# Second MoE: the last group of f made wholly of pairs with seven products

## The chip, the cores and the metric

The program runs on one core of a Trainium2 chip. The metric is the device time of one execution in microseconds (us); lower is better. TensorE (PE in the rows) multiplies matrices into PSUM, VectorE (DVE), ScalarE (ACT) and GpSimd (POOL) work elementwise, and SyncE (SP) issues DMA transfers. PEld is TensorE's loading of weights, which overlaps its matmuls.

## The reference, cut to what matters

Attention with a decay bias makes 2304 tokens of 512 features. Two MoE layers with one expert each follow:

```
def _moe_ref(x, w_in, w_out):
    h = np.maximum(x @ w_in, 0.0)
    return h * h @ w_out                   # 512 -> 2048 -> 512

def _moe2_ref(x, w_in, w_out):
    h = x @ w_in
    g = h * np.cos(h)
    return g @ w_out                       # 512 -> 2048 -> 512
```

The change lies in the second MoE. All is in 32-bit floats at the interface.

## The kernel before, in words

The 2048 hidden columns of the second MoE are 16 chunks f of 128. The 2304 tokens are five blocks j: four of 512 and one of 256 (j = 4). Every 32-bit number that enters a matmul there is split into a high and a low half of 16 bits, and each product is made in three passes (high by high, high by low, low by high).

The chunks are taken in three groups (`GROUPS`). For each group, all blocks are run through one after the other: for each (block, f) the first product makes h in PSUM (`m2_g1`, tile hp, 12 matmuls of 512 columns, or of 256 in the last block), `m2_cos` and `m2_sin` make the cosine (ScalarE: a, kf; VectorE: kf; ScalarE: the sine into a), `m2_mul` multiplies h by it (VectorE), `m2_high` and `m2_rest` split the result into gh (ScalarE) and gl (VectorE), and two items later `m2_g2` multiplies by the second weights and adds up in PSUM (tiles o, one for each 128 tokens). At the end of a group, `m2_g2` evicts each o: the first group's are scaled and stored, the second group's are added by VectorE to what is stored, and the last group's likewise for even tiles, while for odd tiles ScalarE copies into os and GpSimd adds os to the stored part. A group's next o of the same place needs the eviction of the one before.

In the last group (from f = 9), the first f of each block is made as above (an f-item), and the six others as three pairs in the four blocks of 512 (`unit`, from `PAIR0`). A pair makes the first product of two f's in seven products of half the size (`prod`, `PROD`; each six matmuls of 256 columns) in place of the eight that two f's have, as Strassen's and Winograd's methods do: on sums and differences of four quarters of the weights (made once, in `pair_high`: four tensor operations of VectorE into a tile sums, then the high and the low halves) and of the activations (made for each block in `t_make`, a step at each `t_tick`: differences by VectorE, high halves by ScalarE, low halves by VectorE). The products land in three PSUM banks, which share three buffers with hp. ScalarE copies banks into hs (`snap`), VectorE adds banks to hs (`join`). Between the products, `unit` weaves the second products of earlier f's (`out_part`, first and second from a queue `fifo`), and the sines, products and splits of the pair before. Product 5 is accumulated in the bank that `snap` has copied after product 6; product 4 is added in the bank that `join` has read after product 7.

The weights are prepared meanwhile: each chunk is loaded, clipped by ScalarE, put together from bits by two operations of VectorE (`w_bits`), squared for a scale (ScalarE), its scale made (`w_scale`), and split into high (ScalarE) and low halves (VectorE; `w_lo`). How many are taken at each item is set by rates, `P_BITS` first and then `LATE_BITS`; the scales of a group (`group`) must stand before its first f. The order of the instructions on each engine is the order in which this code writes them (the schedule is manual), and each engine takes its own in that order.

Of the kernel before, what the change touches and what calls it, by code (L numbers as in the profile page):

```python
# [8 lines left out]
F32 = mybir.dt.float32  # L9
# [11 lines left out]
DM = 512  # L21
DFF = 2048
KD = DM // 128
NF = DFF // 128
BT = 256
# [2 lines left out]
MAGIC = 12582912.0  # L28
SCALE = 204
TINY = 2.0 ** -96  # L30
GROUPS = ((0, 4), (4, 9), (9, 16))
PAIR0 = 10
T_FROM = 20
LATE_BITS = 0.62
RAWS = 6
NB2 = 5
LAG = (3, 5)
G2LAG = 2
PASSES = ((0, 0), (0, 1), (1, 0))
# [93 lines left out]
def attention_moe_moe_kernel(  # L133
# [18 lines left out]
    nc = tc.nc  # L152
# [38 lines left out]
    p2q = []  # L191
    prog = [0]
    wq = []
    for f in range(NF + G2LAG):
        wq += [(0, f, 0)] if f < NF else []
        wq += [(0, f - G2LAG, 1)] if f >= G2LAG else []
    wq += [(1, f, a) for f in range(PAIR0) for a in range(2)]
    wq += [(1, f + m, a) for f in range(PAIR0, NF, 2) for a in range(2) for m in range(2)]
    spot = {x: j for j, x in enumerate(wq)}

    def home(m, f, a):
# [52 lines left out]
    def v_own(b):  # L254
# [24 lines left out]
        out=ident, in_=ident, pattern=[[-1, 128]], compare_op=ALU.not_equal, fill=1.0,  # L279
# [23 lines left out]
    def store_ones(eng, n0, n1):  # L303
# [10 lines left out]
        out=mask[:, 384:512], in_=mask[:, 384:512], pattern=[[-1, 128]], compare_op=ALU.is_ge,  # L314
        fill=-8.0e9, base=0, channel_multiplier=1,
    )
    for t in early[2:]:
        early_ones(t, nc.gpsimd)
    nc.vector.tensor_scalar(
        out=cs[0:32, 0:S], in0=cs[0:32, 0:S], scalar1=0.0, scalar2=8.0, op0=ALU.max, op1=ALU.mult  # L320
    )
    cc = []
    for x0, x1, t in ((0, BT, "xh"), (BT, S, "xl")):
        nc.vector.tensor_tensor_scan(
            out=c8[0:32, x0:x1], data0=cs[0:32, x0:x1], data1=cs[0:32, x0:x1],
# [51 lines left out]
    for n, (u, b, h, q0, rws, o, nq, nk, nl) in enumerate(heads):  # L377
        q = q0
# [611 lines left out]
    def split(j):  # L990
        return wq[j][0] == 1 and wq[j][1] >= PAIR0 and wq[j][2] == 0

# [17 lines left out]
    def pair_high(j, m):  # L1010

        f = wq[j][1]
        t = wp.tile([128, 2, 512], F32, tag=home(1, f, 0), name="wt3")
        t = t.rearrange("p a c -> p (a c)").bitcast(F16).rearrange("p (e x c) -> p e x c", e=2, x=4)
        sc = sm["wsc"][:, 2 * f:2 * f + 1]
        if m == 0:
            q = p2q[0].tile([128, KD, BT], F32, tag="yr", bufs=2, name="sums")
            x, y = (wst[j + n][1].rearrange("p (a c) -> p a c", a=2) for n in range(2))
            for n, (u, v, op) in enumerate((
                (y[:, 0], y[:, 1], ALU.add), (q[:, 0], x[:, 0], ALU.subtract), (x[:, 0], y[:, 0], ALU.subtract),  # L1020
                (x[:, 1], q[:, 1], ALU.subtract),
            )):
                nc.vector.tensor_tensor(out=q[:, n], in0=u, in1=v, op=op)
            parts = ((t[:, :, 1:3], x), (t[:, :, 0], y[:, 1]), (t[:, :, 3], q[:, 0]))
            wt[1, f, 0] = t[:, :, 1:3].rearrange("p e x c -> p e (x c)")
            pair[f] = (t, y, q)
        else:
            t0, y, q = pair[f - 1]
            parts = ((t[:, :, 0:3], q[:, 1:4]), (t[:, :, 3], y[:, 0]))
            wt[1, f, 0] = (t, t0)  # L1030
            pair[f - 1] = (t0, t)
        pair[j] = (parts, sc)
        for o, i in parts:
            nc.scalar.activation(out=o[:, 0], in_=i, func=ACTF.Copy, scale=sc)
# [20 lines left out]
    stat, part, half, sm = [], {}, {}, {}  # L1055
# [34 lines left out]
    def w_scale(j):  # L1090
# [3 lines left out]
        powers(stat[0][:, c], sm["wsm"][:, c], sm["wex"][:, c], sm["wsc"][:, c])  # L1094
        for g, (f0, f1) in enumerate(GROUPS):
            if wq[j + 1] == (1, f1 - 1, 1):
# [21 lines left out]
    def tables(g, j0, j1):  # L1118

        fs = slice(*GROUPS[g])  # L1120
        n, js = GROUPS[g][1] - GROUPS[g][0], slice(j0, j1)
        nc.vector.scalar_tensor_tensor(
# [109 lines left out]
    yr = {}  # L1232
# [12 lines left out]
    def split_y(j, a):  # L1245
        if a == 0:
            pool = p2q[0] if j < NB2 - 1 else p2q[1]
            yd[j] = [pool.tile([128, KD, blocks[j][1]], F16, tag=f"{x}{j}", bufs=1, name=x) for x in ("yh", "yl")]
# [6 lines left out]
    def load_ys(j):  # L1255
        for a in range(blocks[j][1] // BT if j < NB2 else 0):
            load_y(j, a)
# [28 lines left out]
    def moe_slot():  # L1286
# [9 lines left out]
        g2done[0] += 1  # L1296
        if k == NB1 - 1 and 2 * f >= RAWS and not (f >= PAIR0 and f % 2 == 0):
            while nw[0] < 2 * (NF + f + 1):
# [207 lines left out]
    while prog[0] < unit_done(0):  # L1506
        i = prog[0]
        x = i - FIRST_BITS
        step(bits=int((x + 1) * PROLOG_BITS) - int(x * PROLOG_BITS) if x >= 0 else 0)

    for k in range(NB1):
# [8 lines left out]
        for i in range(J):  # L1520
# [6 lines left out]
            if k == NB1 - 1:  # L1527
# [15 lines left out]
                wlim[0] = 2 * NF + max(RAWS * (i > 1), 2 * max(0, i - LOAD_LAG))  # L1543
                bits = min(2 * GROUPS[0][1], int(max(0, i - 1) * B8_BITS)) - int(max(0, i - 2) * B8_BITS)
                bits = max(0, bits)
# [41 lines left out]
    p2 = ctx.enter_context(tc.tile_pool(name="p2", bufs=1))  # L1587
# [71 lines left out]
    def m2_g2(p, j, f, pick=None):  # L1659
        t0, n = blocks[j]  # L1660
        gh, gl = hd2[j, f]
        w = wt[1, f, 1]
        first, last = (f == x for x in (GROUPS[p][0], GROUPS[p][1] - 1))
        sc = sm["osc"][:, p, j:j + 1]
        if first:
            ops.setdefault(j, {})
        for a in range(n // 128) if pick is None else pick:
            if first:
                ops[j][a] = ps2.tile([128, DM], F32, tag=f"o{a}", name=f"o{a}")
            for m, (e, x) in enumerate(PASSES):  # L1670
                nc.tensor.matmul(  # L1671
                    ops[j][a], (gh, gl)[e][:, a * 128:(a + 1) * 128], w[:, x, :],
                    start=(first and m == 0), stop=(last and m == 2),
                )
            if last:
                st = part[4 * j + a]
                if p == 1 or p and (a % 2 == 0 or j == NB2 - 1):
                    nc.vector.scalar_tensor_tensor(  # L1678
                        out=st, in0=ops[j][a], scalar=sc, in1=st, op0=ALU.mult, op1=ALU.add
                    )  # L1680
                elif p:
                    os = p2.tile([128, DM], F32, tag="os", bufs=2, name="os")
                    nc.scalar.activation(out=os, in_=ops[j][a], func=ACTF.Copy, scale=sc)
                    nc.gpsimd.tensor_tensor(out=st, in0=os, in1=st, op=ALU.add)
                elif a % 2 == 0:
                    nc.scalar.activation(out=st, in_=ops[j][a], func=ACTF.Copy, scale=sc)
                else:
                    nc.vector.tensor_scalar(out=st, in0=ops[j][a], scalar1=sc, scalar2=None, op0=ALU.mult)
            if f == NF - 1:
                for row, x, m in _pieces(t0 + a * 128, 128):  # L1690
                    nc.sync.dma_start(out=out[row:row + m, :], in_=part[4 * j + a][x:x + m])

    HB = BT
    PROD = {1: (0, 1, 0), 2: (0, 2, 1), 3: (1, 2, 2), 4: (0, 0, 6), 5: (0, 3, 3), 6: (1, 0, 4), 7: (1, 1, 5)}
# [90 lines left out]
    def unit(j, f, prev):  # L1785

        p = len(GROUPS) - 1
        w_need(2 * NF + 2 * f + 4)
# [57 lines left out]
    for j in range(NB2):  # L1846
        n = PAIR0 if j < NB2 - 1 else NF
        items += [("f", 2, j, f) for f in range(GROUPS[2][0], n)] + [("u", 2, j, f) for f in range(n, NF, 2)]
    bits0 = nw[2]
    prev = None  # L1850
    for i, (kind, p, j, f) in enumerate(items):
# [22 lines left out]
        if i >= QUIET:  # L1874
            w_squares()
            while wrest:
                x = wrest.pop(0)
# [14 lines left out]
        k = i + 1 - QUIET  # L1892
        goal = min(4 * NF, bits0 + int(max(0, min(k, PAUSE)) * P_BITS) + int(max(0, k - PAUSE - 1) * LATE_BITS))
        if i >= QUIET:
# [17 lines left out]
    while fifo:  # L1912
        m2_g2(*fifo.pop(0))
# [49 lines left out]
```

## Time and profile before

| what | us |
|---|---|
| median of three runs | 971.03 (970.65 to 972.81) |
| profiled execution | 972.91 |
| its span | 970.8 |
| TensorE busy | 937.3 (97%) |
| VectorE busy | 769.7 (79%) |
| ScalarE busy | 709.7 (73%) |
| GpSimd busy | 159.9 (16%) |

The profile is one execution on the chip. The span is the time from its first to its last instruction; the execution lies 2.1 us above it. The second MoE begins at some 595 us: its first products and second products stand in the list of costly groups as lines L1610 (hp) and L1671 (o), the pairs' products as L1762 (bank). The granted TensorE clock is at its full level in all 40 slices of the span.

### The profile page before, as it was taken

What the parts mean: (1) busy time and instruction counts of PE and PEld (TensorE: products, weight loads), DVE (VectorE), ACT (ScalarE), POOL (GpSimd) and SP (SyncE); (2) the same over time, 40 slices, a digit from 0 to 9 for tenths busy, and PEclk for the clock granted to TensorE, in tenths of its full rate; (3) what the DMA queues carried; (4) which work ended last, traced back from release to release, by engine and by line L of the source; (5) the groups of instructions that cost most, each with busy time, mean ns of one, the idle gap of its engine ahead of it and who ended that gap; (6) DMA issues with size and microseconds to landing.
All of it is one profiled execution on the core that took longest, in us unless ns stands there. A gap on an engine that the chain in (4) does not pass through costs nothing.

```text
span 970.8 us, 21039 instructions
## 1 busy us (share of the span) xinstructions
PE 937.3 (97%) x7474; PEld 726.9 (75%) x7474; DVE 769.7 (79%) x1944; ACT 709.7 (73%) x1625; POOL 159.9 (16%) x298
## 2 busy tenths in 40 slices
PE   6999999989999999999999999999999999999997
PEld 5899998988989988999989986445544456666664
DVE  6899986789798866787997375888788788798774
ACT  6799887878898767676776686677777666565553
POOL 2001123222211222222330022430000000001101
PEclk9999999999999999999999999999999999999999
DMA  8984799657998987589999679210000000112001
GB/s 246 312 271 149 168 213 227 168 145 151 200 183 191 204 195 170 134 177 174 211 215 158 217 267 362 66 44 23 1 1 1 22 1 22 49 60 67 23 22 66
DMA packets 158074, 135.38 MB, mean 139 GB/s; under 512 B 109272, under 2 KB 132128, under 8 KB 157968
## 3 DMA queue, kind: packets, MB, share of 16 engines
q1 hardware_dynamic: 147664, 123.78, 50.8%
q0 software_dynamic: 10304, 10.24, 5.2%
q8 instruction: 59, 0.97, 0.4%
q14 instruction: 47, 0.39, 0.1%
HBM read 93.91 MB, written 15.83 MB: 113 GB/s over the span
## 4 chain that ended last, share of the span: by engine, by line
PE 59%; DVE 6%; ACT 3%; issue 2%; DMA 2%; SPq 0%; DVEq 0%; ACTq 0%
PE o L1671 18%; PE hp L1610 12%; PE y L1197 11%; PE hps L1165 9%; PE bank L1762 5%; PE qkp L567 2%; PE pvs L697 2%; DVE k L415 1%; DVE sb L585 1%; DMA raw<-in_qk_dram 1%; DMA rw<-in_w_dram 1%; DMA vb<-v_d 1%; DVE wt L1678 1%; PE xps L752 0%; ACT sb L608 0%
## 5 line engine op out<-in xcount | busy, mean ns | idle before, releaser
L1197 PE MATMUL y<-gh,wt 128*128 128x256 f32 x1152 | 237.7, 289 | 0.0
L1197 PEld LDWEIGHTS y<-gh,wt 128*128 128x128 f32 x1152 | 188.6, 190 | 1.2
L1671 PE MATMUL o<-wt,gh 128*128 128x512 f16 x576 | 171.3, 379 | 1.5 <-ACT gh L1649 1.3
L1197 PE MATMUL y<-gl,wt 128*128 128x256 f32 x576 | 162.9, 283 | 0.5 <-DVE gl L1187 0.5
L1165 PE MATMUL hps<-xh,w 128*128 128x256 f16 x1152 | 142.0, 273 | 2.6 <-ACT g L1177 2.4
L1610 PE MATMUL hp<-yh,wt 128*128 128x512 f16 (+1 forms) x448 | 124.9, 348 | 0.0
L1165 PEld LDWEIGHTS <-w 128*128 128x128 f16 x1152 | 106.1, 98 | 17.8 <-issue 4.2
L1197 PEld LDWEIGHTS y<-gl,wt 128*128 128x128 f32 x576 | 109.9, 191 | 1.4 <-DVE gl L1187 0.9
L1671 PE MATMUL o<-wt,gl 128*128 128x512 f16 x288 | 109.2, 379 | 0.0
L1610 PEld LDWEIGHTS <-wt 128*128 128x128 f16 x672 | 63.9, 98 | 59.1
L1671 PEld LDWEIGHTS <-gh 128*128 128x128 f16 x576 | 56.3, 98 | 56.3 <-ACT gh L1649 1.6
L608 ACT ACTIVATE sb<-sb 128x128 f32<-128x128 f32 (+7 forms) x152 | 87.4, 575 | 4.9 <-DVE sb L585 4.3
L1177 ACT ACTIVATE g<-hps,sc 128x256 f32<-128x256 f32 x96 | 45.1, 470 | 61.3 <-PE hps L1165 59.8
L397 POOL DMA_DIRECT2D k<-ext_d x80 | 41.1, 514 | 260.2 <-PE qkp L567 159.3
L1165 PE MATMUL hps<-xh,wt 128*128 128x256 f32 x384 | 81.4, 294 | 0.3 <-ACT g L1179 0.2
L1187 DVE TENSOR_TENSOR gl<-g,gh 128x256 fp32r<-128x256 f32 x144 | 61.3, 426 | 22.8 <-ACT gh L1181 14.7
L1610 PE MATMUL hp<-yl,wt 128*128 128x512 f16 (+1 forms) x224 | 78.0, 348 | 0.0
L585 DVE CUSTOM_DVE_ANT_0 sb<-qkp,mask 128x128 f32<-128x128 f32 (+7 forms) x152 | 69.3, 456 | 5.3 <-PE qkp L552 4.3
L656 DVE SCALAR_TENSOR_TENSOR p<-sb,p 128x384 f16<-128x384 f32 (+3 forms) x120 | 66.3, 553 | 8.8 <-ACT p L650 5.6
L1635 ACT ACTIVATE a<-kf 128x512 f32<-128x512 f32 (+1 forms) x80 | 46.5, 583 | 31.4 <-DVE kf L1630 30.4
L405 ACT CAST hi<-raw 128x704 fp32r<-128x704 f32 (+2 forms) x80 | 58.8, 735 | 13.6 <-DMA raw<-in_qk_dram 7.2
L1165 PEld LDWEIGHTS hps<-xh,wt 128*128 128x128 f32 x384 | 64.5, 195 | 2.8 <-issue 1.2
(172 smaller groups left out, 2006.8 us busy)
## 6 DMA issues: line engine op xcount, KB each, us to landing
rw<-in_w_dram SPq DMA_DIRECT2D x64, 512.0 KB
raw<-in_qk_dram SPq DMA_DIRECT2D x48, 352.0 KB
yr<-y_d SPq DMA_DIRECT2D x17, 512.0 KB
raw<-in_qk_dram SPq DMA_DIRECT2D x16, 384.0 KB
v_d<-vt SPq DMA_DIRECT2D x16, 320.0 KB
vb<-v_d SPq DMA_DIRECT2D x32, 160.0 KB
vr<-in_v_dram POOLq DMA_DIRECT2D x15, 320.0 KB, 5.4
y_d<-yst SPq DMA_DIRECT2D x18, 256.0 KB
```

What stands on the lines that cost most here:

```text
L405: nc.scalar.copy(hi[:, BT - nq:BT + nk], raw[:, BT - nq:BT + nk])
L585: nc.vector.tensor_tensor_reduce(out=sb[0:r, c0:c0 + cn], in0=p[0:r, 0:cn], in1=mask[0:r, mo:mo + cn], scale=-0.125, scalar=(3.0e38 if k = ...
L608: nc.scalar.activation(out=sb[0:r, 0:w], in_=sb[0:r, 0:w], func=ACTF.Exp, scale=-1.0, bias=j["nb"], accum_out=z[0:r, ti, x:x + 1],)
L656: nc.vector.scalar_tensor_tensor(out=p[0:r, cw:cw + w], in0=sb[0:r, 0:w], scalar=PSC, in1=p[0:r, 0:w], op0=ALU.mult, op1=ALU.subtract,)
L1165: nc.tensor.matmul(hp, w[:, a, c * 128:(c + 1) * 128], (xh, xl)[e][:, c, :], start=(n == 0), stop=(n == 3 * KD - 1),)
L1177: nc.scalar.activation(out=g, in_=hp, func=ACTF.Relu, scale=hs1[:, f // 2:f // 2 + 1])
L1187: nc.vector.tensor_tensor(out=gl, in0=g, in1=gh, op=ALU.subtract)
L1197: nc.tensor.matmul(yps[k][d // 2][:, d % 2, :], w[:, a, d * 128:(d + 1) * 128], (gh, gl)[e], start=(f == 0 and n == 0 and d % 2 == 0), sto ...
L1610: nc.tensor.matmul(hp, chunk_of(w, a, c), (yh, yl)[e][:, c, :], start=(m == 0), stop=(m == 3 * KD - 1),)
L1635: nc.scalar.activation(out=a, in_=kf, func=ACTF.Sin, scale=-6.2831850)
L1671: nc.tensor.matmul(ops[j][a], (gh, gl)[e][:, a * 128:(a + 1) * 128], w[:, x, :], start=(first and m == 0), stop=(last and m == 2),)
L1762: nc.tensor.matmul(bank[b][:, 0:HB], w[:, a, wx, c * 128:(c + 1) * 128], y_side(j, yx, e, c), start=(start and n == 0), stop=(n == 5), ski ...
```

## The change

The groups are now f 0 to 3, 4 to 7 and 8 to 15. The second group so loses f = 8 (five items), and in the last group the four blocks of 512 are made of four pairs each, with no f-item; the block of 256 keeps f-items, eight of them. The weights of the pair (8, 9) are converted with the second ones first, and the rate of conversions late in the first and in the second group goes from 0.62 to 0.76 for each item. The four quarters' sums go into a buffer that they share with os; of os there is so one buffer in place of two. `PARTS` names the tiles in which the 18 results of 128 tokens are kept, since fewer chunks have a tile of that kind.

```diff
-GROUPS = ((0, 4), (4, 9), (9, 16))
-PAIR0 = 10
+GROUPS = ((0, 4), (4, 8), (8, 16))
+PAIR0 = 8
-LATE_BITS = 0.62
+LATE_BITS = 0.76
+PARTS = (*range(2 * PAIR0), 2 * PAIR0 + 1, 2 * PAIR0 + 3)
...
-    wq += [(1, f + m, a) for f in range(PAIR0, NF, 2) for a in range(2) for m in range(2)]
+    wq += [(1, f + m, a) for f in range(PAIR0, NF, 2) for a in ((1, 0) if f == PAIR0 else (0, 1)) for m in range(2)]
...
-            q = p2q[0].tile([128, KD, BT], F32, tag="yr", bufs=2, name="sums")
+            q = p2q[1].tile([128, KD, BT], F32, tag="os", bufs=1, name="sums")
...
-                st = part[4 * j + a]
+                st = part[PARTS[4 * j + a]]
...
-                    os = p2.tile([128, DM], F32, tag="os", bufs=2, name="os")
+                    os = p2.tile([128, KD, BT], F32, tag="os", bufs=1, name="os")[:, 0:2].rearrange("p a c -> p (a c)")
```

The evictions at the end of a block move within the pairs. These are ScalarE's rows around the end of the first block's last group, in the kernel before (os is the copy of an odd o; L1772 the bank copies; L1621 and L1635 make a and the sine, L1649 gh):

```order
L1772 COPY hs<-bank 128x256 x2
L1683 ACTIVATE os<-o_12233,osc 128x512
L1772 COPY hs<-bank 128x256
L1621 ACTIVATE a<-hs,hsc 128x512 x2
L1683 ACTIVATE os<-o_12261,osc 128x512
L1772 COPY hs<-bank 128x256
L1635 ACTIVATE a<-kf 128x512 x2
L1649 CAST gh<-a 128x512
```

and in the change (its lines stand one further down):

```order
L1773 COPY hs<-bank 128x256 x2
L1622 ACTIVATE a<-hs,hsc 128x512 x2
L1773 COPY hs<-bank 128x256
L1684 ACTIVATE os<-o_12082,osc 128x512
L1636 ACTIVATE a<-kf 128x512 x2
L1650 CAST gh<-a 128x512
L1773 COPY hs<-bank 128x256
L1684 ACTIVATE os<-o_12116,osc 128x512
```

Both copies to os moved: the first from behind the earlier bank copies to a place right before the two sines, the second from before them to behind the bank copy that follows gh.

The second place is VectorE early in the second group. Before, behind the product of that group's third item (L1641 is the product, L1708 and L1714 are a difference and a low half of y, L1624 kf, L1656 gl):

```order
L1641 SCALAR_TENSOR_TENSOR a<-hp_11063,gsc,a 128x512
L1708 TENSOR_TENSOR yr<-yr 128x512
L1624 SCALAR_TENSOR_TENSOR kf<-kf,a 128x512
L1656 TENSOR_TENSOR gl<-a,gh 128x512
L1641 SCALAR_TENSOR_TENSOR a<-hp_11108,gsc,a 128x512
L1714 SCALAR_TENSOR_TENSOR wt_9790<-wt_9886,ysc,wt_9790 128x512
```

and in the change the same stretch from the last of the four sums (L1024), which stand behind the same kf, to the next product (L1043 makes a pair's low halves, L982 and L986 the bits):

```order
L1024 TENSOR_TENSOR sums<-st,sums 128x256
L1657 TENSOR_TENSOR gl<-a,gh 128x512
L1043 SCALAR_TENSOR_TENSOR wt_11135<-st,wsc,wt_11135 128x512
L1043 SCALAR_TENSOR_TENSOR wt_11135<-st,wsc,wt_11135 128x256
L1043 SCALAR_TENSOR_TENSOR wt_11135<-sums,wsc,wt_11135 128x256
L982 TENSOR_SCALAR st<-st 128x512
L986 SCALAR_TENSOR_TENSOR st<-rw,st 128x512
L1642 SCALAR_TENSOR_TENSOR a<-hp_11115,gsc,a 128x512
```

The sums and the conversions of the first pair's first half, and two operations on bits, have come in between one item's kf and the next product.

## Rows read from the trace of the kernel before

**Rows 1.** Busy time by stretches: stretch, its length, engines' busy times, PEclk, DMA, GB/s.

```profile
720.00:740.00 20.00, 19.97 (x99) 8.95 (x98) 17.63 (x34) 14.01 (x26) 0.00 (x0) 1.00 0.01 1
800.00:820.00 20.00, 18.21 (x123) 11.65 (x122) 16.51 (x45) 11.63 (x26) 0.00 (x0) 1.00 0.09 27
```

**Rows 2.** Chain of waits from 770 on: start us, us, what.

```profile
772.41 2.61 PE hp L1610 x12
...
824.63 1.30 PE o L1671 x6
825.93 1.31 PE bank L1762 x12
```

**Rows 3.** Timeline, VectorE in the second group, and TensorE's second products by the chain.

```profile
703.39 0.69 DVE L1624 SCALAR_TENSOR_TENSOR kf<-kf,a 128x512 f32<-128x512 f32 x1 [1.29 <-ACT kf L1623]
...
720.16 2.72 DVE L1678 SCALAR_TENSOR_TENSOR wt<-o,osc,wt 128x512 f32<-128x512 f32 x4
...
725.18 0.15 DVE L1076 TENSOR_SCALAR wsm<-stat 128x2 f32<-128x2 f32 x1
...
725.65 0.68 DVE L1624 SCALAR_TENSOR_TENSOR kf<-kf,a 128x512 f32<-128x512 f32 x1
...
726.25 0.42 DVE L1023 TENSOR_TENSOR sums<-st 128x256 f32<-128x256 f32 x1
...
727.71 0.69 DVE L1656 TENSOR_TENSOR gl<-a,gh 128x512 f16<-128x512 f32 x1
728.31 1.15 DVE L1042 SCALAR_TENSOR_TENSOR wt<-st,wsc,wt 128x512 f16<-128x512 f32 x2
...
729.77 0.42 DVE L981 TENSOR_SCALAR st<-st 128x512 int32<-128x512 int32 x1
...
730.83 0.75 DVE L1641 SCALAR_TENSOR_TENSOR a<-hp,gsc,a 128x512 f32<-128x512 f32 x1
...
722.82 2.59 PE o L1671 x12
```

**Rows 4.** Timeline at the passage into the pairs: start us, us, engine, line, operation.

```profile
804.60 1.41 DVE L1051 SCALAR_TENSOR_TENSOR wt<-st,wsc,wt 128x512 f16<-128x512 f32 x2
...
805.92 0.48 DVE L1641 SCALAR_TENSOR_TENSOR a<-hp,gsc,a 128x256 f32<-128x256 f32 x1
...
820.47 0.37 ACT L1772 COPY hs<-bank 128x256 f32<-128x256 f32 x1
...
821.21 0.82 PE L1762 MATMUL bank<-wt,wt 128*128 128x256 f16 x6
```

**Rows 5.** Timeline of a steady pair, from its product 1 to its product 5.

```profile
895.16 0.27 PE L1762 MATMUL bank<-yh,wt 128*128 128x256 f16 x1
...
896.29 1.22 ACT L1635 ACTIVATE a<-kf 128x512 f32<-128x512 f32 x2
...
897.09 1.41 DVE L1641 SCALAR_TENSOR_TENSOR a<-hs,gsc,a 128x512 f32<-128x512 f32 x2
...
897.87 0.62 ACT L1649 CAST gh<-a 128x512 f16<-128x512 f32 x1 [0.35 <-DVE a L1641]
...
898.62 0.37 ACT L1772 COPY hs<-bank 128x256 f32<-128x256 f32 x1
...
900.38 0.82 PE L1762 MATMUL bank<-wt,wt 128*128 128x256 f16 x6
```

**Rows 6.** Timeline: evictions by os, GpSimd's adds, and VectorE beside them.

```profile
882.80 0.69 ACT L1683 ACTIVATE os<-o,osc 128x512 f32<-128x512 f32 x1 [0.98 <-PE o L1671]
...
886.17 1.27 POOL L1684 TENSOR_TENSOR wt<-os,wt 128x512 f32<-128x512 f32 x1 [1.33 <-ACT os L1683]
886.22 1.77 DVE L1630 TENSOR_TENSOR kf<-kf,a 128x512 f32<-128x512 f32 x1
...
951.39 2.50 POOL L1684 TENSOR_TENSOR wt<-os,wt 128x512 f32<-128x512 f32 x2 [29.23 <-ACT os L1683]
...
951.80 0.48 DVE L1641 SCALAR_TENSOR_TENSOR a<-hp,gsc,a 128x256 f32<-128x256 f32 x1
```

More of the change, by code (lines that the diff above doesn't have):

```diff
@@ L1690, in m2_g2 @@
                 for row, x, m in _pieces(t0 + a * 128, 128):
-                    nc.sync.dma_start(out=out[row:row + m, :], in_=part[4 * j + a][x:x + m])
+                    nc.sync.dma_start(out=out[row:row + m, :], in_=part[PARTS[4 * j + a]][x:x + m])
     HB = BT
```

## The prediction, as made before the run

> **What bounds the kernel now.** I read the busy time by stretches first. In the second MoE TensorE works without a break: 19.97 of 20 us between 720 and 740, as in nearly every stretch there; the one poor stretch is 800 to 820, with 18.21 of 20, where the second group of f ends and the pairs begin [rows 1]. So time leaves only with TensorE's columns, and comes with any wait put in front of it. The chain of waits gives the price of each piece of matmul work: an f's first product with 512 tokens is 2.61 us, twelve products of a pair 1.31 us, six matmuls of the second product 1.30 us [rows 2]. The timelines then say how much room the other engines leave, and there lie my other terms.
>
> **Columns.** In each of the four blocks of 512 tokens two f's cost 2 x 2.61 = 5.22 us of first products, and a pair costs 7 x 6 = 42 matmuls of 256 columns, 42/12 x 1.31 = 4.59 us. The pair (8, 9) so gives back 0.63 us a block, 2.5 us in all. The second products stay. The added matmul for the pair's sum of squares and the wider tables of scales are a few rows of some 0.2 us each off TensorE's path. In SP's queue two weight loads change places, long before their weights are used: nothing. The sums' own buffer takes away a sharing with the loads of y; no wait on it shows, so nothing here either.
>
> **Preparing weights in the second group.** The second group has 20 items in place of 25, and the same weights, plus one pair's sums, must be ready before it ends. On VectorE each item has its own work (a product, kf, gl), and the conversions lie between. I walk VectorE's row order of the change from a point where the trace is on time, the kf at 703.39, which waited for ScalarE [rows 3]. Steps are from one start to the next: kf 0.60 (725.65 to 726.25), the four sums 1.46 (to 727.71), gl 0.60, the pair's low halves 1.46 (728.31 to 729.77), bits 1.06 (to 730.83); a product or a low half of y 0.68 (a fourth of the 2.72 of the evictions at 720.16), a difference of y 0.60 as kf, the scales 0.47 (725.18 to 725.65). The order is now: kf, sums, gl, low halves, bits (5.18), product, low, difference (1.96), kf, gl, low halves, bits (3.72), product, low, difference (1.96), kf, gl (1.20), four evictions (2.72), bits (1.06), product, low, scales (1.83), kf, sums, gl to its end (2.75): 22.4 us, to 725.8. TensorE wants that gl as the third matmul of the second products that start at 722.82, at 722.82 + 2 x 0.22 = 723.25. It comes 2.5 us late. Before, the gl for those matmuls stood right before the evictions at 720.16, 3 us before that need, since the pair's sums and their conversions stood later in the order. From below this is 0 (if the row order overlaps more than its starts show; a walk of 42 instructions needs only 0.06 us less on each), from above 4 (two further lags of the kind). I take 2.5, the walk itself.
>
> **The passage into the pairs.** Two f-items disappear between the last weights and the first pair: the block of 256's f = 8 and the first block's f = 9. They gave VectorE time to catch up. The first pair's product 7 needs the PSUM bank that the last f leaves, so it waits for the product that the trace has at 805.92, behind two low halves of weights that take 1.41 from 804.60; the wait is between nothing and these 1.41, and I put 0.8, about the middle, as TensorE meets the rest of the weights' work where it did before. In the second pair product 5 needs a copy of the bank by ScalarE. In the trace that copy ends at 820.47 + 0.37 = 820.84 and product 5 starts at 821.21: room of 0.37 [rows 4]. In the change the second products woven in there are of the block of 256, half as long, so product 5 comes 1.3 us earlier, and an eviction of 0.66 stands before the product that the copy waits behind: 1.3 + 0.66 - 0.37 = 1.6 us. Together 2.4 us; bounds 1 and 3.5.
>
> **The three ends of a block.** In the steady pair product 1 starts at 895.16, and its sines at +1.13, product on VectorE at +1.93, gh at +2.71, bank copy at +3.46 (ends +3.83); product 5 starts at +5.22, so ScalarE may be 1.39 late [rows 5]. Before, an f-item stood between two blocks and the evictions fell behind product 5; a copy to os (0.69) did not stand before a sine of the same pair's chain that TensorE soon needs. Now it does: ScalarE's order is bank copy, os of the second tile, two sines, gh, bank copy, os of the fourth tile. The second tile is finished at +2.62 (1.31 + 1.30), handed over at +2.8, os ends +3.5, the sines +4.1 and +4.7. Then the adder on GpSimd comes in: it starts as os ends and takes 1.27. A VectorE operation with both tensors in SBUF that meets it stands until it is over: kf took 1.77 in place of the 0.69 of the like one [rows 3] and ended 0.55 after GpSimd [rows 6]; a product that reads one tensor from PSUM met another add and took its 0.48. The pairs' product reads two tensors from SBUF, as that kf does. I take it as held: add +3.6 to +4.85, product to +5.4, gh +6.0, bank copy +6.4, so product 5 is 1.15 late.
> The Trainium skill (GPSIMD Engine Reference, section 1, Specifications) says that its SBUF interfaces are shared with VectorE, with contention for operations in a two-port mode or with two SBUF inputs. By it the product is held; no row of before has that pair of operations meeting, and without it product 5 would be 0.6 late by the same walk.
> Behind it the fourth tile's os ends at +7.0, its add holds gl to +8.95, and in the first two ends a difference of y (0.69) and the join (0.42) follow, to +9.9; product 4, wanted at +7.82 (5.22 + 0.65 + 1.30 + 0.65), waits for that join: 2.1 us late. The third end has no difference of y: 1.5. The walk so gives 5.7; I take 5.0, as each wait of TensorE also gives the others time; bounds 1.5 (held by nothing) and 6.5. The last end, into the block of 256, has the two os in one buffer now, so the second waits for the first add (1.27). I assume that TensorE is not waiting for that tile yet and put nothing, with 1.3 as the upper bound.
>
> **Sum.** -2.5 + 2.5 + 2.4 + 5.0 = +7.4 us. The profiled execution took 972.91 (span 970.8), so the same with the change 980.3; the three timed runs' median is 971.03, 1.9 below it, and I forecast 978.4.
>
> **Rivals.** A: TensorE's columns decide and every wait is covered, as in nearly all stretches now. It needs ScalarE's os to be no later than its room of 1.39, and VectorE's walk to be 11% shorter. For it speaks that TensorE waits for next to nothing at 720 to 740 though VectorE is busy 17.63 of 20 us [rows 1]; against it, that the room is measured and the os alone moves the sines by 2.4. The time is 971.03 - 2.5 = 968.5; this is the end on the other side. It decides up to the point where the added waits come to 2.5 us in all.
> B: the product is not held by the add, and the walk in the second group catches up. Then 1.5 to 3 remain of the block ends: -2.5 + 0 + 2 + 2.7 = +2.2, 973.2. For it: the same 17.63 of 20 us leave some room on the mean.
> C: the change prepares too little time: further lags in the second group (up to 4) and the other upper bounds, -2.5 + 4 + 3.5 + 6.5 = +11.5, 982.5. Against it: TensorE's own delays give VectorE time back.
>
> **Chances.** Forecast 0.46, B 0.22, C 0.09, A 0.23. A change under 0.2% (1.9 us) can hardly be told from none; of A and of B some 0.04 each fall there. So faster 0.19, same 0.08, slower 0.73. The forecast's own range is 975.5 to 981. The range from 968 to 982.4 leaves out about a tenth at the lower end and half of C at the upper.
>
> **What would show it.** Right: TensorE idle over 1 us before product 5 and product 4 in the second pair of each block, behind a ScalarE order os, sine, gh; a VectorE product of 1.2 us or more beside GpSimd's add; one gap of 2 us near 725 behind gl; 3 us idle more around the first two pairs. Columns: twelve products of a pair still 1.31. Wrong: the same busy share of TensorE in all stretches from 720 on, and a span 2.5 us shorter, or gaps at places that I have not named.

## The result, and the profile after

The changed kernel takes 979.04 us (median of four runs, 978.38 to 980.78) against 971.50 for the kernel before: 1.0079 times as long, with a 95% interval of 1.0061 to 1.0098. The forecast was 978.4, and slower. The first two parts of the page after, to be held against the small table of before:

```profile
span 976.5 us, 21221 instructions
PE 933.9 (96%) x7548; PEld 730.7 (75%) x7548; DVE 780.5 (80%) x1968; ACT 713.1 (73%) x1639; POOL 160.6 (16%) x298
```

TensorE is busy 3.4 us less and the span is 5.7 us longer, so TensorE stands idle more. Where, the busy time by stretches shows (the columns are those of [rows 1], which show 720 and 800 of before):

```profile
700.00:720.00 20.00, 18.02 (x87) 7.89 (x84) 18.85 (x34) 15.55 (x30) 0.00 (x0) 1.00 0.00 1
720.00:740.00 20.00, 19.93 (x94) 8.99 (x95) 19.04 (x38) 16.72 (x32) 0.00 (x0) 1.00 0.17 53
800.00:820.00 20.00, 20.00 (x136) 13.11 (x134) 16.42 (x29) 12.73 (x24) 0.00 (x0) 1.00 0.10 30
```

VectorE is now busy about 19 of 20 us from 700 to 740, and TensorE loses 2 us there. The stretch from 800 is full, because the pairs begin at 783.57 and no longer at 809.50. The granted clock is full in all three, so the clock has no part in it. (In this execution the granted clock was 0.59 from 24 to 49 us, long before the second MoE, and full from then on.) The view of waits names TensorE's waits from 600 on in the changed kernel (line, tile, what it waited for: total, times, longest). Together they are 12 us.

```profile
PE bank L1763 <- ACT hs L1773: 5.0, 5, 1.5
PE bank L1763 <- DVE hs L1777: 1.9, 3, 0.8
PE stat L1070 <- DVE wsm L1077: 1.6, 1, 1.6
PE o L1672 <- ACT gh L1650: 1.3, 1, 1.3
PE o L1672 <- DVE wt L1679: 0.8, 1, 0.8
PE bank L1763 <- DVE a L1642: 0.5, 1, 0.5
PE o L1672 <- DVE gl L1657: 0.5, 1, 0.5
PE o L1672 <- ACT wt L1712: 0.4, 1, 0.4
```

The kernel before has 2 us:

```profile
PE o L1671 <- ACT gh L1649: 1.3, 1, 1.3
PE bank L1762 <- ACT hs L1772: 0.5, 1, 0.5
PE o L1671 <- DVE wt L1678: 0.2, 1, 0.2
```

To compare kernels I use one number by place, and call it the excess: on TensorE's timeline, the time from the start of one piece of work to the start of the next, less what the piece takes when nothing waits (twelve matmuls of a pair 1.31, six second products 1.30, twelve of these 2.59). It is some 0.16 us larger than the idle gap of the profile at each wait. The lag is the second group up to its last block (in the runs with other rates the waits in the first group are in it), the last items are those of the block of 256, the first two pairs follow, and then come the three ends of a block:

| kernel | lag | last items | first two pairs | three ends | sum |
|---|---|---|---|---|---|
| before | 0.2 | 2.0 | 0.6 | 0.7 | 3.5 |
| changed | 2.4 | 3.4 | 3.2 | 6.0 | 15.0 |

In the profiled executions the second MoE takes 375.6 us before (595.22 to 970.8) and 383.7 after (592.77 to 976.5), 8.1 more: 11.5 of excess, less 2.2 for TensorE's columns, less 1.2 between TensorE's last matmul and the end. It starts 2.45 us earlier in this execution. Between 591.7 and 595.9 that start lies anywhere in the profiles of this study, with no relation to the kernel, so the medians (7.5 us apart) are the better measure of the whole.

**The end of a block.** The timeline of the changed kernel at the end of the first long block, cut to the rows that wait or are waited for:

```profile
833.26 0.69 ACT L1684 ACTIVATE os<-o,osc 128x512 f32<-128x512 f32 x1 [1.58 <-PE o L1672]
833.85 1.14 ACT L1636 ACTIVATE a<-kf 128x512 f32<-128x512 f32 x2
834.03 1.27 POOL L1685 TENSOR_TENSOR wt<-os,wt 128x512 f32<-128x512 f32 x1 [180.18 <-ACT os L1684]
834.50 2.01 DVE L1642 SCALAR_TENSOR_TENSOR a<-hs,gsc,a 128x512 f32<-128x512 f32 x2 [1.14 <-ACT a L1636]
835.88 0.62 ACT L1650 CAST gh<-a 128x512 f16<-128x512 f32 x1 [0.89 <-DVE a L1642]
836.40 0.36 ACT L1773 COPY hs<-bank 128x256 f32<-128x256 f32 x1
836.82 0.81 PE L1763 MATMUL bank<-wt,wt 128*128 128x256 f16 x6 [0.99 <-ACT hs L1773]
837.09 2.35 DVE L1657 TENSOR_TENSOR gl<-a,gh 128x512 f16<-128x512 f32 x2
837.44 1.46 POOL L1685 TENSOR_TENSOR wt<-os,wt 128x512 f32<-128x512 f32 x1 [2.14 <-ACT os L1684]
839.97 0.41 DVE L1777 TENSOR_TENSOR hs<-bank,hs 128x256 f32<-128x256 f32 x1
840.43 0.81 PE L1763 MATMUL bank<-wt,wt 128*128 128x256 f16 x6 [0.82 <-DVE hs L1777]
```

The order of events is the forecast's: os, sines, the add on GpSimd, a pair of products that takes 2.01 in place of the 1.41 of [rows 5], gh, copy, product 5. Then the second add, two gl in 2.35, the join, product 4. In [rows 5] product 5 starts 5.22 us after product 1. Here product 1 starts at 830.46 and product 5 6.36 later.

**The second group.** The timeline of the changed kernel around its longest wait there:

```profile
714.85 2.72 DVE L1679 SCALAR_TENSOR_TENSOR wt<-o,osc,wt 128x512 f32<-128x512 f32 x4
715.64 0.59 PE L1672 MATMUL o<-wt,gh 128*128 128x512 f16 x2 [0.41 <-ACT wt L1712]
719.87 0.15 DVE L1077 TENSOR_SCALAR wsm<-stat 128x2 f32<-128x2 f32 x1
720.07 0.18 PE L1070 MATMUL stat<-wss,onesb 128*128 128x1 bf16 x1 [1.65 <-DVE wsm L1077]
722.40 0.69 DVE L1657 TENSOR_TENSOR gl<-a,gh 128x512 f16<-128x512 f32 x1
```

TensorE waits twice. At 715.64 the row names a ScalarE copy, but what o needs is its buffer: the first of the four evictions ends at 714.85 + 0.68 = 715.53. At 720.07 it waits 1.65 us for a small operation of VectorE on the sums of squares (wsm), which stands behind those evictions, two operations on bits, a product and a low half. The gl of my walk ends at 722.40 + 0.69 = 723.09. The matmul that reads it comes third in the second products that start at 722.70, at 723.1, so after these two waits it is just in time.

The matmul that waits at 720.07 is one column, the sum of squares of the second weights of f = 10 (a pair's first weights have four such matmuls at once, second weights have one each; which it is follows from their order in the code). It is no part of what the change adds. The kernel before has it as well, 5.3 us behind the end of the wsm at 725.18 [rows 3], and there it waits for nothing:

```profile
730.63 0.17 PE L1069 MATMUL stat<-wss,onesb 128*128 128x1 bf16 x1
```

**The passage into the pairs.** The timeline of the changed kernel from the last items to the second pair's product 5:

```profile
773.64 0.39 PE L1672 MATMUL o<-wt,gl 128*128 128x512 f16 x1 [0.52 <-DVE gl L1657]
777.30 2.72 DVE L1679 SCALAR_TENSOR_TENSOR wt<-o,osc,wt 128x512 f32<-128x512 f32 x4
778.10 0.59 PE L1672 MATMUL o<-wt,gh 128*128 128x512 f16 x2 [0.80 <-DVE wt L1679]
785.32 1.41 DVE L1052 SCALAR_TENSOR_TENSOR wt<-st,wsc,wt 128x512 f16<-128x512 f32 x2
786.64 0.48 DVE L1642 SCALAR_TENSOR_TENSOR a<-hp,gsc,a 128x256 f32<-128x256 f32 x1
787.18 0.81 PE L1763 MATMUL bank<-wt,wt 128*128 128x256 f16 x6 [0.53 <-DVE a L1642]
796.20 0.36 ACT L1773 COPY hs<-bank 128x256 f32<-128x256 f32 x1
796.61 0.81 PE L1763 MATMUL bank<-wt,wt 128*128 128x256 f16 x6 [1.47 <-ACT hs L1773]
```

The last two waits are the ones forecast: product 7 behind two low halves and a product, and the second pair's product 5 behind its bank copy. The first two were not: a gl behind the four sums, and evictions that VectorE comes to late.

### The profile page after: what moved, and what is told of

Its sections match the earlier page's. It is cut to its first block, busy times and chain, and to the rows that moved or that the text cites. A ratio compares the mean times of both kernels' runs of the same rounds, so it can differ in the third digit from the quotient of the medians.

```text
span 976.5 us, 21221 instructions
## 1 busy us (share of the span) xinstructions
PE 933.9 (96%) x7548; PEld 730.7 (75%) x7548; DVE 780.5 (80%) x1968; ACT 713.1 (73%) x1639; POOL 160.6 (16%) x298
## 4 chain that ended last, share of the span: by engine, by line
PE 55%; DVE 12%; ACT 4%; DMA 3%; issue 2%; DVEq 0%; POOL 0%; SPq 0%; POOLq 0%; ACTq 0%
PE o L1672 15%; PE y L1198 11%; PE hps L1166 9%; PE hp L1611 8%; PE bank L1763 7%; PE qkp L568 2%; PE pvs L698 2%; DVE wt L1679 1%; DVE gl L1657 1%; DVE a L1642 1%; DMA pt<-p 1%; DMA k<-in_qk_dram 1%; DVE k L416 1%; DVE sb L586 1%; DVE st L986 1%
## 5 line engine op out<-in xcount | busy, mean ns | idle before, releaser
L1611 PE MATMUL hp<-yh,wt 128*128 128x512 f16 (+1 forms) x384 | 104.5, 343 | 0.0
L1611 PEld LDWEIGHTS <-wt 128*128 128x128 f16 x576 | 54.7, 98 | 47.6
L1763 PEld LDWEIGHTS <-wt 128*128 128x128 f16 x672 | 65.7, 98 | 29.9 <-issue 9.9
L1611 PE MATMUL hp<-yl,wt 128*128 128x512 f16 (+1 forms) x192 | 65.9, 343 | 0.0
```

The lines of the kernel that those rows point to most:

```text
L1611: nc.tensor.matmul(hp, chunk_of(w, a, c), (yh, yl)[e][:, c, :], start=(m == 0), stop=(m == 3 * KD - 1),)
L1763: nc.tensor.matmul(bank[b][:, 0:HB], w[:, a, wx, c * 128:(c + 1) * 128], y_side(j, yx, e, c), start=(start and n == 0), stop=(n == 5), ski ...
```

## The experiments

All times are medians, each with its ratio to the kernel before on the same chip; the medians of before lay between 971.1 and 972.4. The excess is that of the profiled execution, by the places of the table above; its sum is rounded by itself.

| run | us | ratio (95% interval) | lag | last items | first pairs | ends | sum |
|---|---|---|---|---|---|---|---|
| changed kernel | 979.04 | 1.0079 (1.0061 to 1.0098) | 2.4 | 3.4 | 3.2 | 6.0 | 15.0 |
| e1_no_add | 976.07 | 1.0042 (1.0025 to 1.0059) | 2.4 | 3.4 | 3.2 | 1.9 | 11.0 |
| e2_os_late | 978.18 | 1.0066 (1.0043 to 1.0089) | 2.4 | 3.4 | 3.2 | 4.4 | 13.4 |
| e3_tfrom28 | 979.92 | 1.0081 (1.0057 to 1.0105) | 1.6 | 3.7 | 3.2 | 6.0 | 14.5 |
| e4_pair10 | 971.46 | 1.0000 (0.9984 to 1.0016) | 0.1 | 3.8 | 1.4 | 0 | 5.3 |
| e5_before_buf | 970.76 | 0.9991 (0.9976 to 1.0006) | 0.2 | 2.0 | 0.6 | 0.5 | 3.3 |
| h1_evict | 975.64 | 1.0038 (1.0024 to 1.0052) | 2.4 | 3.4 | 3.2 | 1.9 | 10.9 |
| h2_order | 976.02 | 1.0044 (1.0030 to 1.0058) | 2.4 | 3.4 | 3.1 | 2.0 | 11.0 |
| p1_pace | 978.86 | 1.0075 (1.0057 to 1.0093) | 3.2 | 1.8 | 3.3 | 6.0 | 14.3 |
| m1_first | 974.00 | 1.0028 (1.0017 to 1.0039) | 2.4 | 3.4 | 1.4 | 1.9 | 9.0 |
| m2_tfrom26 | 974.13 | 1.0025 (1.0009 to 1.0042) | 2.1 | 3.9 | 1.4 | 1.9 | 9.3 |
| m4_pace | 975.09 | 1.0032 (1.0020 to 1.0043) | 2.4 | 3.1 | 1.4 | 1.9 | 8.8 |
| m5_both | 973.79 | 1.0025 (1.0005 to 1.0045) | 1.9 | 3.9 | 1.4 | 1.9 | 9.1 |

### Which part of the change costs the time

**Groups as changed, pairs from 10** (e4_pair10).

```diff
-PAIR0 = 8
+PAIR0 = 10
```

> Groups of f, rate and buffers as changed, but the pairs begin at f = 10 as before, so f 8 and 9 are f-items at the head of each long block of the last group. Theory (the waits come from the pair (8, 9): no f-items at block ends and at the passage, and one more pair to prepare): TensorE has 2.5 us more of columns than the changed kernel, the block ends fall from 6.0 to about 0.7, the lag in the second group (2.4) goes, the passage falls from 6.7 to about 2.7: time 979.0 + 2.5 - 5.3 - 2.4 - 4.0 = 969.8, at most 972. Rival (the shorter second group itself, or the shared buffer of os and sums, makes the waits): 975 or more.

Without the pair (8, 9) the time is that of the kernel before. (At this `PAIR0` the pair (10, 11) takes the reversed order of its weights.) All of TensorE's waits from 600 on:

```profile
PE o L1672 <- DVE wt L1679: 1.4, 2, 0.8
PE o L1672 <- ACT gh L1650: 1.3, 1, 1.3
PE o L1672 <- DVE gl L1657: 0.7, 2, 0.5
PE bank L1763 <- ACT hs L1773: 0.5, 1, 0.5
```

The waits at product 5 and at the join at the ends are gone, and the lag with them; so these come with the pair. What stays is the last items, 3.8 of excess in place of the 2.0 of before. These come without the pair, with the shorter second group or the rates that were changed with it; this run has both, and p1_pace below shows that the rates alone move them. The theory had put the last items and the first pairs at 2.7 together; they are 5.2. That the time is no longer than before all the same has to do with the end of the program, which is 1.2 us shorter in this run, as in the changed kernel.

**The buffer alone** (e5_before_buf): the kernel before, with sums and os in one buffer.

```diff
-            q = p2q[0].tile([128, KD, BT], F32, tag="yr", bufs=2, name="sums")
+            q = p2q[1].tile([128, KD, BT], F32, tag="os", bufs=1, name="sums")
...
-                    os = p2.tile([128, DM], F32, tag="os", bufs=2, name="os")
+                    os = p2.tile([128, KD, BT], F32, tag="os", bufs=1, name="os")[:, 0:2].rearrange("p a c -> p (a c)")
```

> The kernel before, with one part of the change alone: the four sums in one buffer shared with os, and one buffer of os in place of two; groups, pairs and rates as before. Theory (the shared buffer costs nothing; all of the loss comes from the pair (8, 9)): no wait of TensorE is added, time within 0.2% of the kernel before, 971 to 973 by a median of 972.4. Rival (the second os waits for the first add, or the sums wait for it): 1 to 3 us at the three block ends, 974 or more.

The interval holds 1. The buffer costs nothing, as forecast.

### The ends of a block

**No add on GpSimd** (e1_no_add). Left out are the adds of os, so the parts of the output that need them are incomplete; there are eight in all, the six at the three ends of a block and two of the fourth long block, made when the block of 256 has begun. The expectation counts six.

```diff
-                    nc.gpsimd.tensor_tensor(out=st, in0=os, in1=st, op=ALU.add)
```

> The changed kernel without GpSimd's six adds of os to the stored part in the last group's four long blocks (so six of the output's 18 parts lack that sum); ScalarE still makes the copies. Theory (the add holds VectorE's operations with two SBUF inputs, as kf was held to 1.77 us): the first product of the pair at a block's end falls from 1.3 us to 0.75, product 5 waits 0.6 in place of 1.0, and product 4 no longer waits for the join; the three ends fall from 6.0 us above undisturbed spacing to 1.8, and the time from 979.0 to about 975. Rival (only ScalarE's order and VectorE's own load make the waits): the waits at product 5 and product 4 stay as they are, time 978.5 to 979.5.

The same rows of this run's timeline, at the end of its first block:

```profile
836.96 1.42 DVE L1642 SCALAR_TENSOR_TENSOR a<-hs,gsc,a 128x512 f32<-128x512 f32 x2 [1.13 <-ACT a L1636]
838.27 0.36 ACT L1772 COPY hs<-bank 128x256 f32<-128x256 f32 x1
838.69 0.81 PE L1762 MATMUL bank<-wt,wt 128*128 128x256 f16 x6 [0.40 <-ACT hs L1772]
838.96 1.50 DVE L1657 TENSOR_TENSOR gl<-a,gh 128x512 f16<-128x512 f32 x2
```

The two products take 1.42 in place of 2.01 and the two gl 1.50 in place of 2.35. Product 5 waits 0.40 (excess 0.56 at each end, 0.6 was expected), product 4 for nothing. The time is 976.07, where about 975 was expected. Of the 6.0 us at the ends, 4.1 come from VectorE being held by an engine that is 16% busy, and 1.9 stay, nearly all of it product 5's wait behind ScalarE's order. The product reads two tensors from SBUF and is held; rival B is refuted in that. The Trainium skill (SBUF — State Buffer, section "SBUF: two separate sides") says that the port pair that the two engines share is an exclusive lock between a GpSimd operation and one of VectorE that runs in a two-port mode or has two inputs in SBUF (the latter against a GpSimd operation that reads SBUF, as the add does): whichever starts first has it for the whole instruction, and the other one blocks. The rows agree in both directions: VectorE's products stand while the add runs, and in the changed kernel the second add began while gl was running and took 1.46 in place of 1.27.

**Copies to os later** (e2_os_late). The odd tiles' evictions are kept in a list and written behind the bank copy, and behind the second gh.

```diff
...
         snap(j, f, 0, 1, 0)
+        evict_late()
         prod(j, f, 7, 2, True)
         out_part(first, 1)
         if old:
             m2_high(*old[1])
+            evict_late()
```

> The changed kernel with both copies to os put later on ScalarE: the first behind the bank copy that frees product 5, the second behind the second gh. Theory (order of ScalarE sets product 5, the GpSimd add sets product 4): the wait at product 5 (1.0 us) goes at all three ends; the adds now meet the two gl of the pair, hold them, and the join behind them is about 1.7 us late, so product 4 takes over most of it: block ends 4.5 to 5.5 us in place of 6.0, time about 978. Rival (the copy before the sines is the whole cause, and product 4 is late only because product 5 was): both waits go, 6.0 falls below 1, time about 973.5.

```profile
837.40 2.15 DVE L1657 TENSOR_TENSOR gl<-a,gh 128x512 f16<-128x512 f32 x2
839.00 0.39 PE L1684 MATMUL o<-wt,gl 128*128 128x512 f16 x1 [0.57 <-DVE gl L1657]
839.47 1.75 DVE L1720 TENSOR_TENSOR yr<-yr 128x512 f32<-128x512 f32 x1
841.61 0.81 PE L1774 MATMUL bank<-wt,wt 128*128 128x256 f16 x6 [0.76 <-DVE hs L1788]
```

Product 5 waits no more. The first add now holds the first gl (the two gl take 2.15 in place of the 1.50 of e1_no_add), and the second add, which itself comes behind the second gl, holds the difference of y (1.75 in place of 0.68). TensorE waits for the first gl and then for the join: 1.8 us at an end in place of 2.2. At the third end there is no difference of y, the join meets the add and is not held, and product 4 waits for nothing. So the ends are 4.4, just under the 4.5 to 5.5 expected. As the theory had it, a copy moved out of one chain puts its add in front of another. I had named the join alone; the second products that read gl came in between.

**Evictions shared out otherwise** (h1_evict). VectorE evicts the first two tiles at once; ScalarE and GpSimd take the last two, one behind the join and one a product later, and that pair's difference of y goes behind the join.

```diff
...
-                if p == 1 or p and (a % 2 == 0 or j == NB2 - 1):
+                if p == 1 or p and (a < 2 or j == NB2 - 1):
...
         join(j, f, 2, 1, 1)
+        if late:
+            t_tick(j + 1)
+        evict_late(1)
         out_part(second, 0)
         t_tick(j + 1)
         prod(j, f, 3, 0, False)
         snap(j, f, 0, 0, 1)
+        evict_late()
```

> The changed kernel with the evictions at a block's end shared out otherwise: the first two tiles by VectorE at once, the last two by ScalarE and GpSimd, and those only behind the join that product 4 waits for; that pair's difference of y behind the join too. Theory (product 5 waits for os before the sines and for the product that the add holds, product 4 for a join behind gl held by the add): the ends fall from 6.0 us above undisturbed spacing to 0.5 to 1.5, time about 975 by a median before of 972.4 (ratio 1.003). Rival (VectorE has no room for one more eviction ahead of the products): the wait at product 5 stays about 1 us an end, time 977.5 or more.

The ends fall to 1.9 us, somewhat above the 0.5 to 1.5 expected, and the time to 975.64, as expected. The 1.9 is a new wait, 0.77 (excess 0.93) at each of the first two ends: a second product needs the tile whose os stands behind the first add in the one buffer. The rival, that VectorE had no room, is refuted.

### The lag and the passage

**Copy before gh** (h2_order), on top of the run before:

```diff
+        snap(j, f, 0, 1, 0)
         if old:
             m2_high(*old[0])
             m2_mul(*old[1])
-        snap(j, f, 0, 1, 0)
...
-            m2_rest(*old[1])
-            t_tick(j + 1)
...
+        if old:
+            m2_rest(*old[1])
+            t_tick(j + 1)
```

> As the run with the evictions shared out otherwise, and in every pair ScalarE copies the bank that product 5 waits for before the first gh, and VectorE makes the second gl and the difference of y behind the join. Theory (product 5 waits for the chain of sine, product and gh only because the copy stands behind gh): the 1.6 us at product 5 of the second pair goes too, but gl of the pair before is late there by 0.5 to 1.3, so 0.3 to 1 us less than that run, about 974.5. Rival (nothing stands before the copy but the chain of the bank itself): the same time as that run.

```profile
795.79 0.60 PE L1684 MATMUL o<-wt,gh 128*128 128x512 f16 x2 [0.51 <-DVE a L1642]
797.06 0.39 PE L1684 MATMUL o<-wt,gl 128*128 128x512 f16 x1 [0.67 <-DVE gl L1657]
```

The 1.6 us at the second pair's product 5 are gone, and 1.5 have come back at the two waits shown. The order of the copy was what held product 5, and yet nothing is gained: the second products want gh and gl, which end the same chain of sine, product and gh, and that chain is late in this pair. The time is 976.02, no less than that of the run it is made from, as the rival had it, though not for the rival's reason.

**F-items in the first block** (m1_first), on top of h1_evict:

```diff
-        n = PAIR0 if j < NB2 - 1 else NF
+        n = PAIR0 + 2 * (j == 0) if j < NB2 - 1 else NF
...
-        w_need(2 * NF + 2 * f + 2)
+        w_need(2 * NF + 2 * f + 2 + 2 * (p == 2 and f == PAIR0))
```

> The version with the evictions shared out otherwise, and in the first long block of the last group f 8 and 9 are f-items again (from the pair's own tiles of weights); the blocks behind keep that pair. Theory (without an f-item between the last weights and the first pair VectorE cannot catch up): the passage falls from 6.7 us above undisturbed spacing to 3 to 5.3 (2.65 in the kernel before, 5.2 in the version whose pairs begin at 10), TensorE has 0.63 us more of columns: 0.8 to 3 us less than the version it is made from, 972.5 to 975 by a median before of 971.6. Rival (the passage's waits come from the conversions of the second group alone): they stay and the time rises by 0.6, to 976.3.

The first pairs fall from 3.2 to 1.4. With 0.6 us more of columns that is a gain of some 1.3 us on the version it is made from; the ratio goes from 1.0038 to 1.0028, with intervals that overlap, so the time alone does not show it. In the trace TensorE waits no more at product 7 and at the second pair's product 5 (one wait of 0.6 for an eviction has come in, as in the run with pairs from 10). So those two waits do come from the missing f-items. The last items keep their 3.4, and with pairs from 10 they kept 3.8.

**Thinning VectorE's work** (e3_tfrom28, p1_pace, and on top of m1_first m2_tfrom26, m4_pace and m5_both). One number or two are changed in each: where the differences of y begin, and the rates of conversion in the first and in the second group.

```diff
 e3_tfrom28: T_FROM 20 -> 28
 p1_pace: P_BITS 0.75 -> 0.90, LATE_BITS 0.76 -> 0.66
 m2_tfrom26: T_FROM 20 -> 26
 m4_pace: P_BITS 0.75 -> 0.85, LATE_BITS 0.76 -> 0.74
 m5_both: as m4_pace, T_FROM 20 -> 27
```

> The changed kernel with the first block's differences of y (four differences and four low halves of VectorE, 5.1 us) begun at item 28 in place of item 20. Theory (VectorE is behind in the second group by some 2.4 us and TensorE meets that lag at the first wait it comes to): the waits near 712 to 720 go, 2.4 us; but the last items of the group and the passage get the 5.1 us, so the excess there rises from 6.7 by 0 to 3 us: time 976.5 to 979.5. Rival (the matmul for the pair's sum of squares waits for its own chain, whatever VectorE does besides): 1.6 us stay at that matmul and the time is 979 or more.

> The changed kernel with two conversions of weights moved from the second group to the first (rates 0.90 and 0.66 in place of 0.75 and 0.76; the last stands at the same item). Theory (VectorE's lag in the second group is a matter of total work there, 97% busy from 701 to 740 against 82% from 593 to 701, and a conversion takes 2.5 to 2.9 us of VectorE): the lag of 2.4 us goes, the waits of the last items fall by up to 2, the first group shows at most 1 us: time 2.5 to 4 us below the changed kernel, about 976.5 by a median before of 972.4. Rival (the waits hang on where single operations stand in the order, as with the difference of y moved later): they turn up at other items and the time stays within 1 us of the changed kernel, 979 to 981.

> As the run with f-items in the first block, and the first block's differences of y begun at item 26 in place of 20. Theory (total work of VectorE decides, and there are now two f-items more to take it): the lag of 2.4 us near 715 falls below 1, the passage grows by 0 to 1.5: 0 to 1.5 us less than that run. Rival (single places in the order decide): waits turn up elsewhere, within 0.5 us of that run.

> As the run with f-items in the first block, with rates of 0.85 and 0.74, so that the last conversion of weights stands before the second group's last block. Theory: the lag near 715 falls from 2.4 to about 1.5, the last items of the group lose 1 to 2 us of waits, the first group shows up to 1 us: 1 to 2.5 us less than that run, 971 to 973.5. Rival (the waits only move, as with the other rates tried): within 0.7 us of that run.

> As the run with f-items in the first block and rates 0.85 and 0.74, and the first block's differences of y begun at item 27. Theory (each lag is VectorE's work of one stretch, so thinning both crowded stretches must help where thinning one only moved it): waits above undisturbed spacing fall from 8.9 us in all to 6.5 to 8, time 973 to 974 by a median before of 971.1. Rival (single places decide): 8.5 to 9.5 us remain, 974.5 to 975.5. Either way it stays above the kernel before.

None of the five gained so much that it can be told from nothing. In e3_tfrom28, with the differences of y begun later, two of the changed kernel's rows of waits have become:

```profile
PE o L1672 <- DVE gl L1657: 1.0, 3, 0.5
PE stat L1070 <- DVE wsm L1077: 0.4, 1, 0.4
```

The wait at the sum of squares shrinks from 1.6 to 0.4, against that run's rival, which had it stay (its expectation calls this matmul the pair's; it is the single one named above). A wait of 0.5 near 760 and two for gl take its place, and the time is not shorter. The rates of p1_pace halve the last items (3.4 to 1.8), and a wait of 1.1 at the end of the first group and waits of 1.0 and 0.2 near 724 come instead. My theory in these runs, that the loss goes once VectorE's total work in a stretch is thinned, is not borne out: the sums of the excess change by 0.7 us or less against the versions that the runs are made from, mostly because the waits moved, though in the changed kernel VectorE is busy only 88.2 of the 108.1 us from 592.8 to 700.9. The last run is mixed: m5_both's time of 973.79 lies in the theory's range, its 9.1 us of waits in the rival's. Whether some other order of the second group has no such waits is open; these five do not show it.

No version beats the kernel before: the best of those with the pair (8, 9) are 0.25% above it.

## Why the prediction was right

The forecast was 978.4 and the median is 979.04; the steps, in the prediction's order:

- **Columns:** -2.5 forecast. The second MoE up to TensorE's last matmul, less the excess, fell from 367.1 to 364.9 us, by 2.2.
- **Buffer:** nothing forecast, nothing found (e5_before_buf).
- **Second group:** 2.5 forecast from a walk along VectorE's rows; the excess grew by 2.2. (In the timeline of before the matmul that wants this gl starts at 723.08 and not at 723.25, so the walk itself gives 2.7.) The walk was sound: it put the end of gl at 725.8, which is 723.4 with the second MoE 2.45 us earlier, and it ended at 723.09. The place was wrong: I took this gl for the next thing that TensorE wants from VectorE. A one-column matmul for a sum of squares, which stands in TensorE's queue in both kernels and which I had not put on the walk, wants VectorE's wsm earlier. I had set aside the added matmuls of that kind as off TensorE's path, and this is not even one of the added. Its wait (1.65) and one for an eviction (0.41) came before gl, and had made up the lag when gl was wanted.
- **Passage:** 2.4 forecast, bounds 1 to 3.5; the growth was 4.0, beyond the upper bound. The two waits I named came as sized: products 6 and 7 are 1.0 late (0.8), the second pair's product 5 is 1.6 late (1.6). The step that failed is that they were the only ones: the last items lost 1.4 us more. I had taken TensorE to meet the rest of the weights' work where it did before; by the run with pairs from 10 that part comes without the pair, with the shorter second group or its rates.
- **Ends of a block:** 5.0 taken, 5.7 by the walk less what the trace of before loses there. The growth was 5.3. Product 5 is 1.15, 1.22 and 1.22 late (1.15 forecast), and up to product 4 it is 2.2, 2.2 and 1.6 (2.1, 2.1, 1.5, the last 1.4 by the walk's own steps). The hold by GpSimd's add, which no row of before had for this pair of operations, is what e1_no_add shows.
- **The last end:** nothing forecast, no wait there.
- **Not forecast:** the program ends 3.8 us after TensorE's last matmul in place of 5.0. The run with the buffer alone has 4.9, and every other run, all with the new groups, 3.8. The traces show one difference: in the two profiles with 5.0 and 4.9 one DMA packet of 8 KB of the kind "instruction" runs some 2.6 us after TensorE's last matmul, before the last store has landed, and in the other twelve none runs there. No run changes this alone, so the cause stays open.

The sum was +7.4: corrected by +0.3 (columns), -0.3 (second group), +1.6 (passage), +0.3 (ends) and -1.2 (end of the program) it is 8.1, which is the second MoE's growth in the profiles. The two larger errors, the last items and the end of the program, nearly cancelled, so the closeness of the total is in part luck. Of the signs named ahead, VectorE's product beside the add came (1.34 us for the held one), and product 5 waited 1.0 at each end; product 4 waited 0.8, 0.8 and 0.2 and not over 1, and the gap near 725 came as two, earlier and not behind gl. Rival A, every wait covered, needed added waits of 2.5 us in all; they are 11.5.

## What to carry to other kernels

Where an engine in the middle runs close to the bottleneck, saving work on the bottleneck takes away its slack as well: count what the removed items gave the others time for, and walk the order of each of them, row by row, up to the next thing that the bottleneck wants. In such a walk put every instruction of the bottleneck's queue on the path, however small, since in its queue a matmul of one column stops it as a large one does. And an operation that costs its own engine nothing can hold another's: look at what runs beside GpSimd before putting work there.

## What the hardware showed

GpSimd's add also holds an operation of VectorE with one tensor read, if that is the quick tensor_scalar. In h1_evict, one add and the operation beside it:

```profile
841.21 1.27 POOL L1668 TENSOR_TENSOR wt<-os,wt 128x512 f32<-128x512 f32 x1 [0.80 <-ACT os L1667]
841.77 0.99 DVE L1630 TENSOR_SCALAR kf<-a 128x512 f32<-128x512 f32 x1 [0.48 <-ACT a L1622]
```

This tensor_scalar takes 0.42 us where no add runs, against the 0.69 us of the operations with two inputs of the same size. Here it took 0.99, and ended 0.28 after the add. The product that reads PSUM and met an add in [rows 6] was not held, so it is the kind of the operation, not the engine, that decides.

The thirteen profiles that have these adds say the same throughout, for the operations of VectorE that start while an add runs: 46 with two inputs in SBUF (products, gl, kf, differences and low halves of y) all end 0.55 us after the add, 37 of this tensor_scalar end 0.15 (256 columns) to 0.29 us (512) after it, and 27 with an input in PSUM keep the time that they have alone.
